# Attention and two expert layers in one kernel: the stores of weight operands leave SP's queue one slot later, behind the reads of transposed probabilities

## The chip, the cores and the metric

The kernel runs on one core of a Trainium2 chip. The metric is the time of one execution in microseconds (us), of which a lower one is better. Three runs of the kernel before gave a median of 992.63 us (991.09 to 993.33).

The engines are named as the profile names them: PE multiplies matrices (PEld is its weight load), DVE, ACT and POOL work on vectors, SP issues nearly all DMAs. SP's queue is served in order: an issue that waits holds up all issues behind it.

## The reference

The reference chains three parts. Attention in chunks of 32 queries over 8 memory keys and a window of keys (16 to the left, 8 to the right), for 4 batches, 8 heads, 768 positions, 64 numbers per head; then a layer with a cosine gate; then a layer with the maximum of three products.

```python
scores = scale * np.matmul(q_c, k_full.transpose(0, 1, 3, 2))
a = np.exp(scores - np.max(scores, axis=-1, keepdims=True))
a = a / (np.sum(a, axis=-1, keepdims=True) + 1e-09)
out[:, :, c_start:c_end] = np.matmul(a, v_full)
...
h = x @ w_in                    # 3072 x 512 by 512 x 2048
g = h * np.cos(h)
x = g @ w_out                   # back to 512
...
h = np.maximum(np.maximum(x @ w1, x @ w2), x @ w3)   # 512 to 768
return h @ w_out2
```

## The kernel before, in words

**Operands.** An fp32 product is made of three passes: each operand is split into a high part (an ACT copy to a shorter type) and the rest (a subtraction on DVE or POOL), and PE adds high by high, high by rest and rest by high (`PASSES`, `products`, line 393). So each weight needs an ACT and a DVE or POOL instruction before PE can use it, and the pair is 512 KB.

**Blocks and slots.** The 3072 tokens are 6 blocks of 512 (`j`). A block has 16 slots (`f`), one for each 128 hidden units of the first layer. In slot `s`, PE first makes `h` of that slot (`p1`, 12 matmuls). Then `chain` turns `h` into `g`: ACT (line 451), DVE (453, 454), ACT's sine (456), DVE (458), ACT (462), POOL (463); in block 0 a slightly different chain (lines 430 to 448). Then PE adds the product of `g` of slot `s - 2` with `w_out` into four banks `acc` (`p2`, 12 matmuls, in early slots of block 0 four). `g` thus has two slots of time to come about.

**Attention rides along.** While block `j` is in its slots, the attention of block `j + 1` is computed, in four units of 128 queries (numbers 0 to 3). The steps of a unit are put into slots by three tables of strings: `FIRST` for block 0, `SECOND` for block 1, `STEADY` for blocks 2 to 4. A string such as `9: "V0 T1 N2"` says what is done in slot 9:

- `S`: scores (`a_scores`, 16 + 16 matmuls, line 246, two banks of the pool `ps_a`), mask and maximum on DVE, and the load of a later unit's q and k;
- `E`: two units' exponentials on ACT (with a table load);
- `N`: row sums and reciprocals on DVE, the scaling on POOL (line 282);
- `T` (`a_t`): a DVE transpose in 32 x 32 squares (line 286, 0.97 us), and a store of the 384 KB to memory (`ptd`, line 287);
- `L` or `l` (`a_l`): three DMAs (line 292) that read them back from `ptd` in the order that PE needs, into the tile `pt`. There is one buffer for `pt`, so a load waits until the `V` before it has read it;
- `V` (`a_v`): the product with v (line 306, 16 + 16 matmuls into one bank `s`), its split into the block's `x` on ACT (308) and DVE (309), and the load of a later v (line 239).

There are two buffers in `ps_h` (tag `h`) and two in `ps_a` (tag `a`); `h` of a slot lies in `ps_h`. In `SECOND` the bank of `V` comes from `ps_h`, elsewhere from `ps_a`.

**Stores of weight operands.** `w_split` (line 203 on) splits w_in and w_out in block 0, two weights in a slot, and stores eight of the pairs (`wad`, line 211), since the buffers don't hold all 16; `wa_fetch` (line 412) brings them back in each later block. From slot 27 on, `prep_go` prepares the second layer's weights (nine groups of four operands, `q_split`, and six of `w_out2`, `o_steps`), through `store` (lines 542 to 546): ACT copy, DVE or POOL subtraction, DMA to `wd` or `wod`. `store` takes its tile from the pool `pre`, which has four buffers that also hold the group's two raw weights. Blocks of the second layer (`quad`, `b_out`) follow after slot 95 and fetch `wd` and `wod`.

**What sets the order.** A function `slot(s)` calls everything in the order of a slot: `wa_fetch`, `p1`, `chain` (with the `T` and `L` of the slot as its argument `turned`, called behind the DVE step that ends the use of `h`), and then `S`, `E`, `N`, `l` and `V` of the table with `p2`. PE and SP execute in exactly this order (`keep`, `hold`); on DVE, ACT and POOL a scheduler may move instructions that aren't kept in place. An SP issue of line 211 or 546 stands where the split is called, so it waits for the DVE or POOL instruction just ahead of it.

Of the kernel before, what the change touches and what calls it, by code (L numbers as in the profile page):

```python
# [9 lines left out]
F32 = mybir.dt.float32  # L10
# [21 lines left out]
ND = NB * S // (2 * QU)  # L32
# [3 lines left out]
DB = N // (2 * QU)  # L36
# [10 lines left out]

FIRST = {2: "S0", 3: "S1", 4: "S2", 5: "S3 E01", 6: "E23 N0", 7: "T0 N1", 8: "L0", 9: "V0 T1 N2", 10: "L1 N3", 11: "V1 T2", 12: "L2 T3", 13: "V2 l3", 14: "V3"}  # L50
SECOND = {0: "S0", 1: "S1", 2: "E01 S2", 3: "N0", 4: "S3 T0", 5: "E23 N1 L0", 6: "V0 S4 N2", 7: "T1", 8: "L1 N3", 9: "V1 S5 T2", 10: "L2 E45", 11: "V2 S6 T3", 12: "L3", 13: "V3 S7", 14: "E67"}
STEADY = {1: "N0", 2: "T0 N1", 3: "L0", 4: "S4", 5: "V0 T1 N2", 6: "L1", 7: "S5", 8: "V1 T2 N3", 9: "L2 E45", 10: "S6 T3", 11: "V2 l3", 12: "S7", 13: "V3", 14: "E67"}


# [23 lines left out]
def attn_moe_kernel(ctx, tc, qT, kT, vw, w_in, w_out, w3, w2o, out):  # L78
# [3 lines left out]
    keep = tc.keep_in_program_order  # L82
# [118 lines left out]
    def w_split(key, eng):  # L201
        c = wst.pop(key)
        w = wp.tile([128, 2, 512], F32R, tag="w", name="w")
        live[0] += 1
        assert live[0] <= NW
        keep(ACT.activation(out=w[:, 0, :], in_=c, func=AF.Copy))
        keep(eng.tensor_tensor(w[:, 1, :], c, w[:, 0, :].bitcast(F32), op=ALU.subtract))  # L207
        live[0] -= key[0] != "out" or key[1] >= PLAIN or key[1] % 2 and key[1] < PLAIN - 1
        DST[key[0]][key[1]] = (w[:, 0, :], w[:, 1, :])
        if key[0] == "out" and key[1] >= RES:  # L210
            SP.dma_start(out=wad[key[1]], in_=w.rearrange("p a c -> p (a c)").bitcast(F32))


    qk, vt, ss, sm, pt = {}, {}, {}, {}, {}
# [69 lines left out]
    def a_t(d):  # L284
        m = sm[d]
        keep(DVE.transpose(m, m))
        keep(SP.dma_start(out=ptd[d % 2], in_=m))
# [7 lines left out]
    def a_v(d):  # L295
        p, v = pt[d], vt[d]
        j, o = divmod(d, DB)
        if o == 0:
            xT[j] = xp.tile([128, 2, 4, N], F32R, tag="x", name="x")
        x = xT[j][:, :, :, 128 * o:128 * o + 128]  # L300
        late = not 2 * DB <= d < 3 * DB
        s = (ps_a if late else ps_h).tile([128, 4, 128], F32, tag="a" if late else "h", name="s")
        for t in range(2):
            for h in range(H):
                p0 = 64 * (h % 2)
                keep(PE.matmul(s[p0:p0 + 64, h // 2, QU * t:QU * t + QU], lhsT=v[:KU, t, 64 * h:64 * h + 64],  # L306
                               rhs=p[:KU, 2 * (h % 2):2 * (h % 2) + 2, 4 * t + h // 2, :], start=True, stop=True))
        ACT.activation(out=x[:, 0], in_=s, func=AF.Copy)
        DVE.tensor_tensor(x[:, 1], s, x[:, 0].bitcast(F32), op=ALU.subtract)
# [85 lines left out]
    def p1(j, f):  # L395
        if f % 2 and (done[0] or j == 0 and f == 1):
            h = ps_a.tile([128, N], F32, tag="a", name="h")
        else:
            h = ps_h.tile([128, N], F32, tag="h", name="h")
        w, x = wA_in[f], xT[j]  # L400
        for k in range(4):
            products(h, w, k, [x[:, i, k, :] for i in range(2)], k == 0, k == 3)
        live[0] -= j == NBLK - 1
        hq[j, f] = h
# [20 lines left out]
    def chain(j, f, fill, turned):  # L425
        h = hq.pop((j, f))
        ki = tr.tile([128, N], I32, tag="r", name="ki")
        c = ki.bitcast(F32)
        if j == 0:
            ACT.activation(out=ki, in_=h, func=AF.Copy, scale=INV2PI)  # L430
            DVE.scalar_tensor_tensor(c, h, INV2PI, ki, op0=ALU.mult, op1=ALU.subtract)
            fill("d0")
            fill("a0")
            ACT.activation(out=c, in_=c, func=AF.Sin, scale=math.pi)
            ACT.activation(out=c, in_=c, func=AF.Square)
            fill("a1")
            if f < PLAIN:
                g = g_t[j, f] = g_tile(F32)
                DVE.scalar_tensor_tensor(g[:, 0, :], c, 0.5, h, op0=ALU.subtract, op1=ALU.mult)
                for fn, d in turned:  # L440
                    fn(d)
            else:
                g = g_t[j, f] = g_tile()
                DVE.scalar_tensor_tensor(c, c, 0.5, h, op0=ALU.subtract, op1=ALU.mult)
                for fn, d in turned:
                    fn(d)
                ACT.activation(out=g[:, 0, :], in_=c, func=AF.Copy)
                POOL.tensor_tensor(g[:, 1, :], c, g[:, 0, :].bitcast(F32), op=ALU.subtract)
            fill("z")
            return  # L450
        row(ACT.activation(out=ki, in_=h, func=AF.Copy, scale=INV2PI, bias=0.25))  # L451
        fill("a0")
        row(DVE.scalar_tensor_tensor(c, h, INV2PI, ki, op0=ALU.mult, op1=ALU.subtract))  # L453
        row(DVE.tensor_scalar(c, c, -0.75, 0.25, op0=ALU.max, op1=ALU.min))  # L454
        fill("d0")
        row(ACT.activation(out=c, in_=c, func=AF.Sin, scale=2 * math.pi, bias=pio2))  # L456
        fill("a1")
        row(DVE.tensor_tensor(c, h, c, op=ALU.mult))  # L458
        for fn, d in turned:
            fn(d)  # L460
        g = g_tile()
        row(ACT.activation(out=g[:, 0, :], in_=c, func=AF.Copy))  # L462
        row(POOL.tensor_tensor(g[:, 1, :], c, g[:, 0, :].bitcast(F32), op=ALU.subtract))  # L463
        fill("z")
        g_t[j, f] = g
# [70 lines left out]
    def q_split(q, i, eng):  # L536
# [2 lines left out]
        n = 512 if i < 3 else 256  # L539
        store(src, n, eng, wd[q][i])  # L540

    def store(src, n, eng, dst):
        w = pre.tile([128, 2, n], F32R, tag="p", name="wq")
        keep(ACT.activation(out=w[:, 0, :], in_=src, func=AF.Copy))  # L544
        keep(eng.tensor_tensor(w[:, 1, :], src, w[:, 0, :].bitcast(F32), op=ALU.subtract))  # L545
        keep(SP.dma_start(out=dst, in_=w.rearrange("p a c -> p (a c)").bitcast(F32)))

    def q_fetch(p, q):
        for i in range(4):
# [322 lines left out]
    def slot(s):  # L872
        j, f = slots[s]
# [12 lines left out]
        def fill(where):  # L886
# [19 lines left out]
            elif where == "z":  # L906
                dec.bits()
                dec.exp(dec.nb + 2)
                dec.load()

        while wf[0] < min(s + (3 if s >= turn else 2), total):
            wa_fetch(*slots[wf[0]])
            wf[0] += 1
        p1(j, f)
        moved = [op for op in todo if op[0] in "TL" and base + int(op[1:]) < ND]
        chain(j, f, fill, [((a_t, a_l)["TL".index(op[0])], base + int(op[1:])) for op in moved])

        def do2():
            while n2[0] <= s - LOOK:
# [35 lines left out]
    for s in range(total):  # L955
        if s == turn:
            att_cm.__exit__(None, None, None)
            tmp_open("ph2", 2)
            done[0] = True
        slot(s)  # L960
        if s < PINNED:
            hold()
        else:
            hold(only=(PE.engine, SP.engine) if s < turn else (PE.engine,))
    hold(False)
    got = [AHEAD]

# [98 lines left out]
```

## Time and profile before

| | |
|---|---|
| median of 3 runs | 992.63 us (991.09 to 993.33) |
| profiled execution, its own time | 992.27 us |
| span of the profiled execution | 990.5 us |
| PE busy | 968.6 us (98%), 5426 matmuls |
| DVE busy | 555.8 us (56%) |
| ACT busy | 440.4 us (44%) |
| POOL busy | 394.4 us (40%) |
| mean granted clock of PE | 0.998 of full speed |
| moved by DMA | 186.01 MB, 188 GB/s |

The profile is of one execution; its own time is 1.77 us more than its span, and 0.36 us under the median. "Busy" is summed over instructions. A row of a timeline gives the start, the length, engine, line, operation and tiles, and in brackets how long the engine had been idle and what ended that. An idle time that is put down to a DMA is the time until its data had landed.

### The profile page before, as it was taken

The page shows a single profiled execution, that of the slowest core. Times are in us where ns is not written, and L with a number is a line of the kernel's source. Part 1 is how long each engine was busy: PE and PEld are TensorE (multiplying, and loading weights), DVE is VectorE, ACT ScalarE, POOL GpSimd, SP SyncE. Part 2 cuts the span into 40 slices and gives each one's busy share as a digit, 9 for nine tenths or more (in the row PEclk, how much of TensorE's full clock was granted, in tenths as well). Part 3 has the DMA queues.
Part 4 walks back from the last instruction along what each step waited for, and adds up shares of the span by engine and source line. Part 5 has one row for each costly group of instructions (what it writes and reads, how often), then busy time and mean ns, then how long its engine had stood idle before and what let it go on. Part 6 is the DMA issues. An engine that isn't in the chain of part 4 may idle for free.

```text
span 990.5 us, 14443 instructions
## 1 busy us (share of the span) xinstructions
PE 968.6 (98%) x5426; PEld 781.4 (79%) x5427; DVE 555.8 (56%) x840; ACT 440.4 (44%) x758; POOL 394.4 (40%) x314
## 2 busy tenths in 40 slices
PE   8998999999999999989999999999999999999998
PEld 5665778788888788878888888888888888888886
DVE  7687846564667656656655464545371455524440
ACT  6566645545445554455544454433242333323320
POOL 3565435443354445355442233333351343324320
PEclk9999999999999999999999999999999999999999
DMA  9985543456557754773577467586625655165101
GB/s 256 338 314 191 176 133 119 139 168 183 192 177 231 251 191 149 221 242 125 178 242 259 153 223 276 168 320 202 203 84 196 207 185 198 74 235 181 42 22 65
DMA packets 67413, 186.01 MB, mean 188 GB/s; under 512 B 7568, under 2 KB 15504, under 8 KB 67344
## 3 DMA queue, kind: packets, MB, share of 16 engines
q1 hardware_dynamic: 67200, 184.96, 56.1%
q8 instruction: 43, 0.70, 0.3%
q14 instruction: 26, 0.21, 0.1%
q10 hardware_dynamic: 144, 0.13, 0.0%
HBM read 140.76 MB, written 44.30 MB: 187 GB/s over the span
## 4 chain that ended last, share of the span: by engine, by line
PE 80%; DVE 6%; DMA 4%; ACT 4%; issue 3%; POOL 1%; SPq 1%; ACTq 0%; POOLq 0%; DVEq 0%
PE hb L690 26%; PE h L393 21%; PE acc L393 17%; PE hb L788 10%; DMA pt<-ptd 3%; PE s L246 2%; PE s L306 2%; PE acc L390 1%; DMA v<-in_vw_dram 1%; DVE raw L198 1%; SPq L292 1%; DVE w L207 1%; DVE ki L458 1%; DVE ki L453 1%; POOL g L463 1%
## 5 line engine op out<-in xcount | busy, mean ns | idle before, releaser
L393 PE MATMUL h<-x,w 128*128 128x512 f32 x1152 | 284.8, 397 | 1.9 <-DVE ki L458 1.9
L393 PEld LDWEIGHTS h<-x,w 128*128 128x128 f32 x1152 | 214.5, 189 | 50.9 <-DVE ki L458 2.2
L463 POOL TENSOR_TENSOR g<-ki,g 128x512 fp32r<-128x512 f32 x80 | 107.2, 1339 | 230.7 <-ACT g L462 197.0
L690 PE MATMUL hb<-x,wq 128*128 128x512 f32 x648 | 155.6, 389 | 0.0
L690 PEld LDWEIGHTS hb<-x,wq 128*128 128x128 f32 x648 | 121.6, 188 | 25.3
L393 PE MATMUL acc<-g,w 128*128 128x512 f32 x576 | 138.4, 389 | 0.0
L393 PEld LDWEIGHTS acc<-g,w 128*128 128x128 f32 x576 | 108.1, 188 | 22.5
L690 PE MATMUL hb<-xo,wq 128*128 128x512 f32 x486 | 119.1, 389 | 0.0
L393 PE MATMUL acc<-g,wa 128*128 128x512 f32 x480 | 115.9, 390 | 1.6 <-POOL g L463 1.6
L393 PEld LDWEIGHTS acc<-g,wa 128*128 128x128 f32 x480 | 89.9, 188 | 21.1 <-POOL g L463 2.5
L690 PEld LDWEIGHTS hb<-xo,wq 128*128 128x128 f32 x486 | 91.2, 188 | 18.9
L456 ACT ACTIVATE ki<-ki,pio 128x512 f32<-128x512 f32 x80 | 57.9, 723 | 106.8 <-DVE ki L454 106.7
L788 PE MATMUL hb<-wo,g 128*128 128x512 f32 x432 | 98.4, 389 | 0.0
L453 DVE SCALAR_TENSOR_TENSOR ki<-h,ki 128x512 f32<-128x512 f32 x80 | 55.0, 687 | 72.5 <-ACT ki L451 72.4
L788 PEld LDWEIGHTS hb<-wo,g 128*128 128x128 f32 x432 | 81.1, 188 | 16.8
L714 POOL TENSOR_TENSOR p<-p,p 128x512 f32<-128x512 f32 x27 | 34.8, 1290 | 130.6 <-ACT p L711 130.6
L458 DVE TENSOR_TENSOR ki<-h,ki 128x512 f32<-128x512 f32 x80 | 55.2, 690 | 56.1 <-ACT ki L456 56.1
L462 ACT ACTIVATE g<-ki 128x512 fp32r<-128x512 f32 x80 | 50.5, 631 | 58.9 <-DVE ki L458 58.9
L451 ACT ACTIVATE ki<-h 128x512 int32<-128x512 f32 x80 | 47.1, 589 | 63.2 <-PE h L393 57.8
L714 DVE TENSOR_TENSOR a<-a,hb 128x512 f32<-128x512 f32 x27 | 18.6, 688 | 93.8 <-PE hb L690 93.8
L545 DVE TENSOR_TENSOR wq<-raw,wq 128x512 fp32r<-128x512 f32 x33 | 41.2, 1266 | 24.8 <-ACT wq L544 23.5
L198 DVE SCALAR_TENSOR_TENSOR raw<-raw,top 128x512 int32<-128x512 int32 x48 | 44.2, 920 | 18.4 <-ACT top L181 13.3
(113 smaller groups left out, 1115.2 us busy)
## 6 DMA issues: line engine op xcount, KB each, us to landing
wq<-wd SPq DMA_DIRECT2D x81, 512.0 KB, 4.7
wa<-wad SPq DMA_DIRECT2D x40, 512.0 KB, 5.9
wd<-wq SPq DMA_DIRECT2D x27, 512.0 KB, 2.7
v<-in_vw_dram SPq DMA_DIRECT2D x24, 384.0 KB, 5.3
raw<-in_w_dram SPq DMA_DIRECT2D x18, 511.8 KB, 5.9
raw<-in_w_in_dram SPq DMA_DIRECT2D x16, 511.8 KB, 10.2
raw<-in_w_out_dram SPq DMA_DIRECT2D x16, 511.8 KB, 10.2
k<-in_kT_dram SPq DMA_DIRECT2D x24, 320.0 KB, 4.6
```

The source lines that it names most:

```text
L198: keep(DVE.scalar_tensor_tensor(o, z, 13, top[key], op0=ALU.logical_shift_right, op1=ALU.bitwise_or))
L393: PE.matmul(o, lhsT=w[a][:, sl], rhs=x[b], start=first and n == 0, stop=last and n == 2)
L451: row(ACT.activation(out=ki, in_=h, func=AF.Copy, scale=INV2PI, bias=0.25))
L453: row(DVE.scalar_tensor_tensor(c, h, INV2PI, ki, op0=ALU.mult, op1=ALU.subtract))
L456: row(ACT.activation(out=c, in_=c, func=AF.Sin, scale=2 * math.pi, bias=pio2))
L458: row(DVE.tensor_tensor(c, h, c, op=ALU.mult))
L462: row(ACT.activation(out=g[:, 0, :], in_=c, func=AF.Copy))
L463: row(POOL.tensor_tensor(g[:, 1, :], c, g[:, 0, :].bitcast(F32), op=ALU.subtract))
L545: keep(eng.tensor_tensor(w[:, 1, :], src, w[:, 0, :].bitcast(F32), op=ALU.subtract))
L690: keep(PE.matmul(o, lhsT=w[:, a, 256 * half + 128 * c:256 * half + 128 * c + 128], rhs=x[c][:, b, :], start=first and n == 0, stop=n == 5, ...
L714: keep(eng.tensor_tensor(o, a, b, op=op))
L788: keep(PE.matmul(o, lhsT=g[:, i, 128 * m:128 * m + 128], rhs=w[k], start=(f == 0 and n == 0), stop=(f == FB - 1 and n == 2)))
```

## The change

Four things are changed.

1. `a_l` of the table's `L` is called at the start of its slot, ahead of `wa_fetch` and `p1`, instead of within `chain`. `l` stays behind `V`.
2. The DMA of a weight store isn't issued where the operand is split, but put on a list, `later`; `flush()` issues the list in the next slot, behind that slot's `L` and `wa_fetch` and ahead of `p1` (and a last time after the last slot).
3. In `FIRST` and `SECOND` steps are moved by one to three slots, and in `FIRST` `L1` and `L2` become `l1` and `l2`. `STEADY` is as before.
4. `V` takes its bank from `ps_a` in all blocks.

```diff
-FIRST = {2: "S0", 3: "S1", 4: "S2", 5: "S3 E01", 6: "E23 N0", 7: "T0 N1", 8: "L0", 9: "V0 T1 N2", 10: "L1 N3", 11: "V1 T2", 12: "L2 T3", 13: "V2 l3", 14: "V3"}
-SECOND = {0: "S0", 1: "S1", 2: "E01 S2", 3: "N0", 4: "S3 T0", 5: "E23 N1 L0", 6: "V0 S4 N2", 7: "T1", 8: "L1 N3", 9: "V1 S5 T2", 10: "L2 E45", 11: "V2 S6 T3", 12: "L3", 13: "V3 S7", 14: "E67"}
+FIRST = {2: "S0", 3: "S1", 4: "S2", 5: "S3 E01", 6: "E23 N0", 7: "T0 N1", 8: "L0 T1 N2", 9: "V0 l1 T2", 10: "V1 l2 N3", 11: "T3", 12: "V2 l3", 14: "V3"}
+SECOND = {0: "S0", 1: "S1", 2: "E01 S2", 3: "N0 S3", 4: "T0", 5: "E23 N1 L0 S4", 6: "V0 T1", 7: "L1 N2", 8: "S5 T2 N3", 9: "V1 E45", 10: "L2 S6 T3", 11: "V2", 12: "L3 S7", 13: "V3", 14: "E67"}
 STEADY = {1: "N0", 2: "T0 N1", 3: "L0", 4: "S4", 5: "V0 T1 N2", 6: "L1", 7: "S5", 8: "V1 T2 N3", 9: "L2 E45", 10: "S6 T3", 11: "V2 l3", 12: "S7", 13: "V3", 14: "E67"}
...
         if key[0] == "out" and key[1] >= RES:
-            SP.dma_start(out=wad[key[1]], in_=w.rearrange("p a c -> p (a c)").bitcast(F32))
+            later.append((wad[key[1]], w.rearrange("p a c -> p (a c)").bitcast(F32)))
...
-        late = not 2 * DB <= d < 3 * DB
-        s = (ps_a if late else ps_h).tile([128, 4, 128], F32, tag="a" if late else "h", name="s")
+        s = ps_a.tile([128, 4, 128], F32, tag="a", name="s")
...
+    later = []
+
+    def flush():
+        while later:
+            out, in_ = later.pop(0)
+            keep(SP.dma_start(out=out, in_=in_))
...
         keep(eng.tensor_tensor(w[:, 1, :], src, w[:, 0, :].bitcast(F32), op=ALU.subtract))
-        keep(SP.dma_start(out=dst, in_=w.rearrange("p a c -> p (a c)").bitcast(F32)))
+        later.append((dst, w.rearrange("p a c -> p (a c)").bitcast(F32)))
...
+        for op in todo:
+            if op[0] == "L" and base + int(op[1:]) < ND:
+                a_l(base + int(op[1:]))
         while wf[0] < min(s + (3 if s >= turn else 2), total):
             wa_fetch(*slots[wf[0]])
             wf[0] += 1
+        flush()
         p1(j, f)
-        moved = [op for op in todo if op[0] in "TL" and base + int(op[1:]) < ND]
-        chain(j, f, fill, [((a_t, a_l)["TL".index(op[0])], base + int(op[1:])) for op in moved])
+        chain(j, f, fill, [base + int(op[1:]) for op in todo if op[0] == "T" and base + int(op[1:]) < ND])
```

What this does to the order, at three places.

SP in block 0, from the store of unit 0's transpose on (`ptd_108` and `ptd_109` are the two buffers in memory, used in turn; `raw` are loads of weights). Before:

```order
L287 DMA ptd_108<-sm 128x768
L169 DMA raw<-in_w_in_dram 128x2047
L169 DMA raw<-in_w_out_dram 128x2047
L211 DMA wad_100<-w 128x1024
L292 DMA pt<-ptd_108 32x4x256 x3
L169 DMA raw<-in_w_in_dram 128x2047
L169 DMA raw<-in_w_out_dram 128x2047
L211 DMA wad_101<-w 128x1024
L287 DMA ptd_109<-sm 128x768
L239 DMA v<-in_vw_dram 96x1024
L211 DMA wad_102<-w 128x1024
L292 DMA pt<-ptd_109 32x4x256 x3
```

and now:

```order
L287 DMA ptd_108<-sm 128x768
L169 DMA raw<-in_w_in_dram 128x2047
L169 DMA raw<-in_w_out_dram 128x2047
L292 DMA pt<-ptd_108 32x4x256 x3
L287 DMA ptd_109<-sm 128x768
L169 DMA raw<-in_w_in_dram 128x2047
L169 DMA raw<-in_w_out_dram 128x2047
L546 DMA wad_100<-w 128x1024
L287 DMA ptd_108<-sm 128x768
L239 DMA v<-in_vw_dram 96x1024
L292 DMA pt<-ptd_109 32x4x256 x3
```

The reads of `pt` of units 0 and 1 no longer stand behind a `wad` store; the store of unit 1's transpose has moved ahead of two weight loads, and that of unit 2 ahead of unit 1's read.

SP in block 2, from the store of unit 3's transpose to its read (`wd_0` to `wd_3` are one group of the second layer's operands). Before:

```order
L287 DMA ptd_109<-sm 128x768
L546 DMA wd_0_118<-wq 128x1024
L230 DMA q<-in_qT_dram 128x512
L231 DMA k<-in_kT_dram 128x640
L412 DMA wa<-wad_104 128x1024
L546 DMA wd_1_119<-wq 128x1024
L546 DMA wd_2_120<-wq 128x1024
L239 DMA v<-in_vw_dram 96x1024
L292 DMA pt<-ptd_109 32x4x256 x3
L412 DMA wa<-wad_105 128x1024
```

and now:

```order
L287 DMA ptd_109<-sm 128x768
L230 DMA q<-in_qT_dram 128x512
L231 DMA k<-in_kT_dram 128x640
L411 DMA wa<-wad_104 128x1024
L546 DMA wd_0_118<-wq 128x1024
L239 DMA v<-in_vw_dram 96x1024
L292 DMA pt<-ptd_109 32x4x256 x3
L411 DMA wa<-wad_105 128x1024
L546 DMA wd_1_119<-wq 128x1024
L546 DMA wd_2_120<-wq 128x1024
```

Two stores, `wd_1` and `wd_2`, have moved from ahead of the read to behind it, and `wd_0` stands nearer to it. `STEADY` is unchanged, so this is `flush` alone.

PE in block 1 at unit 0's `V` (line 306, 305 in the changed kernel) and the scores of the unit after the next (line 246). Before:

```order
L393 MATMUL h<-x,w 128x512 x12
L393 MATMUL acc_1623<-g,w 128x512 x3
L393 MATMUL acc_1624<-g,w 128x512 x3
L393 MATMUL acc_1625<-g,w 128x512 x3
L393 MATMUL acc_1626<-g,w 128x512 x3
L306 MATMUL s<-pt,v 64x64 x16
L246 MATMUL s<-k,q 64x96 x16
L393 MATMUL h<-x,w 128x512 x12
```

and now:

```order
L246 MATMUL s<-k,q 64x96 x16
L392 MATMUL h<-x,w 128x512 x12
L392 MATMUL acc_1623<-g,w 128x512 x3
L392 MATMUL acc_1624<-g,w 128x512 x3
L392 MATMUL acc_1625<-g,w 128x512 x3
L392 MATMUL acc_1626<-g,w 128x512 x3
L305 MATMUL s<-pt,v 64x64 x16
L392 MATMUL h<-x,w 128x512 x12
```

The scores stand a slot ahead of `V` instead of right behind it. PE's instructions are the same in number and size throughout; only such steps change places.

## Rows read from the trace of the kernel before

**Rows 1.** The page's head and its first row on PE (section 1).

```profile
span 990.5 us, 14443 instructions
PE 968.6 (98%) x5426; PEld 781.4 (79%) x5427; DVE 555.8 (56%) x840; ACT 440.4 (44%) x758; POOL 394.4 (40%) x314
```

**Rows 2.** Waits of PE over the span: us in total, times, longest us.

```profile
PE s L306 <- DMA pt<-ptd: 8.7, 7, 2.8
PE h L393 <- DVE ki L458: 1.9, 2, 1.3
PE acc L393 <- POOL g L463: 1.6, 2, 1.3
```

**Rows 3.** Timeline of PE in block 0: V0 to V3, and h after V0.

```profile
93.55 1.15 PE L306 MATMUL s<-pt,v 96*64 96x64 f32 x32 [2.82 <-DMA pt<-ptd]
94.63 4.62 PE L393 MATMUL h<-x,w 128*128 128x512 f32 x12
...
108.34 1.15 PE L306 MATMUL s<-pt,v 96*64 96x64 f32 x32 [0.91 <-DMA pt<-ptd]
...
121.19 1.15 PE L306 MATMUL s<-pt,v 96*64 96x64 f32 x32 [0.59 <-DMA pt<-ptd]
...
129.15 1.15 PE L306 MATMUL s<-pt,v 96*64 96x64 f32 x32 [1.13 <-DMA pt<-ptd]
```

**Rows 4.** Busy time by stretch, granted clock (PEclk), DMA share, GB/s: block 0.

```profile
90.00:100.00 10.00, 7.18 (x50) 5.30 (x49) 4.63 (x6) 3.68 (x7) 3.97 (x4) 0.83 0.83 282
91.00:130.00 39.00, 33.83 (x245) 27.44 (x247) 29.05 (x33) 23.51 (x41) 17.49 (x15) 0.96 0.68 224
```

**Rows 5.** Timeline of PE in blocks 1 to 3: stalls, and h after the longest.

```profile
184.83 3.02 PE L393 MATMUL h<-x,w 128*128 128x512 f32 x12 [1.26 <-DVE ki L458]
...
229.97 1.15 PE L306 MATMUL s<-pt,v 96*64 96x64 f32 x32 [0.55 <-DMA pt<-ptd]
...
331.55 1.15 PE L306 MATMUL s<-pt,v 96*64 96x64 f32 x32 [0.84 <-DMA pt<-ptd]
...
434.30 1.15 PE L306 MATMUL s<-pt,v 96*64 96x64 f32 x32 [1.88 <-DMA pt<-ptd]
435.38 3.02 PE L393 MATMUL h<-x,w 128*128 128x512 f32 x12
```

**Rows 6.** Timeline of SP in block 0.

```profile
81.50 0.33 SPq L287 DMA_DIRECT2D ptd<-sm  x1
...
88.02 0.33 SPq L211 DMA_DIRECT2D wad<-w  x1
88.45 1.74 SPq L292 DMA_DIRECT2D pt<-ptd  x3
...
122.84 0.37 SPq L239 DMA_DIRECT2D v<-in_vw_dram  x1
123.39 1.63 SPq L292 DMA_DIRECT2D pt<-ptd  x3
```

**Rows 7.** DMA issues: KB each, median us from issue to landing.

```profile
ptd<-sm SPq DMA_DIRECT2D x20, 384.0 KB, 2.6
wd<-wq SPq DMA_DIRECT2D x27, 512.0 KB, 2.7
```

**Rows 8.** Timeline of DVE in block 0: transpose of unit 1.

```profile
90.62 0.97 DVE L286 STREAM_TRANSPOSE sm<-sm 128x768 f32<-128x768 f32 x1
```

**Rows 9.** Timeline of SP in block 2, ahead of unit 3's read.

```profile
323.02 1.34 SPq L546 DMA_DIRECT2D wd<-wq  x2
...
324.90 2.01 SPq L292 DMA_DIRECT2D pt<-ptd  x3
```

**Rows 10.** ACT's copy of an operand to be stored: count, busy, mean ns, idle before.

```profile
L544 ACT ACTIVATE wq<-raw 128x512 fp32r<-128x512 f32 x33 | 20.9, 655 | 2.9 <-DVE raw L198 1.6 <-POOL raw L522 1.0 <-issue 0.4
```

**Rows 11.** Timeline of POOL in block 3: a g.

```profile
399.47 1.29 POOL L463 TENSOR_TENSOR g<-ki,g 128x512 fp32r<-128x512 f32 x1 [2.51 <-ACT g L462]
```

**Rows 12.** Timeline of PE in block 3: the product that uses this g.

```profile
406.85 2.88 PE L393 MATMUL acc<-g,wa 128*128 128x512 f32 x12
```

More of the change, by code (lines that the diff above doesn't have):

```diff
@@ L439, in chain @@
                 DVE.scalar_tensor_tensor(g[:, 0, :], c, 0.5, h, op0=ALU.subtract, op1=ALU.mult)
-                for fn, d in turned:
-                    fn(d)
+                for d in turned:
+                    a_t(d)
             else:
@@ L444, in chain @@
                 DVE.scalar_tensor_tensor(c, c, 0.5, h, op0=ALU.subtract, op1=ALU.mult)
-                for fn, d in turned:
-                    fn(d)
+                for d in turned:
+                    a_t(d)
                 ACT.activation(out=g[:, 0, :], in_=c, func=AF.Copy)
@@ L458, in chain @@
         row(DVE.tensor_tensor(c, h, c, op=ALU.mult))
-        for fn, d in turned:
-            fn(d)
+        for d in turned:
+            a_t(d)
         g = g_tile()
@@ L964, in attn_moe_kernel @@
             hold(only=(PE.engine, SP.engine) if s < turn else (PE.engine,))
+    flush()
     hold(False)
```

## The prediction
> **What bounds the kernel now.** I read the page first: PE is busy for 968.6 of 990.5 us [rows 1], and the change leaves the number and sizes of its matmuls alone. So only PE's idle time can be won, 21.9 us in all, together with stretches in which its clock is low. I then asked for PE's waits [rows 2]: 8.7 us for `pt` ahead of `V`, 1.9 us for DVE ahead of `h`, 1.6 us for POOL's g; the rest of the idle time lies in the start-up and at the end, where nothing is changed. Then I looked up each stall in PE's timeline: four ahead of `V0` to `V3` in block 0, of 2.82, 0.91, 0.59 and 1.13 us [rows 3], and one each in blocks 1, 2 and 3, of 0.55, 0.84 and 1.88 us [rows 5]. The longest has a sequel: the 12 matmuls of `h` behind it took 4.62 us [rows 3] against 3.02 us elsewhere [rows 5], which is 1.60 us more, and the mean granted clock of those ten microseconds was 0.83 [rows 4], so part of them ran at 1.2 instead of 2.4 GHz. No other stall has such a sequel; the `h` behind the stall of 1.88 us took 3.02 us [rows 5]. Last, SP's timeline says why the reads are late. In block 0 the transpose was on its way at 81.50, but the read left at 88.45, right behind the `wad` store at 88.02, which had waited for its DVE split [rows 6].
>
> **The change, part by part.** The profiled execution took 992.27 us, 0.36 us less than the median of the runs, so I work out a difference and take it from the median.
>
> *V0 in block 0.* The read now stands ahead of the `wad` store. The transpose's store left at 81.50 and a store of this kind lands after 2.6 us [rows 6, 7], so the read can leave at 84.1 instead of 88.45. From the first issue to the start of `V0` it was 93.55 - 88.45 = 5.1 us [rows 3, 6], so the data is there at 89.2. PE was free at 93.55 - 2.82 = 90.73. The stall goes, with 1.5 us to spare, and the slow clock that followed it: 2.82 + 1.60 = 4.42 us.
>
> *V1 in block 0* moves from slot 11 to slot 10, one slot behind `V0`. Its read can only leave once `V0` has emptied the single `pt` buffer, and the load of v stands ahead of it. That is what `V3` had before: the `V` ahead of it ended at 121.19 + 1.15 = 122.34, v left at 122.84, the read at 123.39, and `V3` began at 129.15, after a stall of 1.13 us [rows 3, 6]. So the old stall of 0.91 us goes and one of some 1.13 us comes. Its lower bound is 0; its upper one is `V0`'s old loss, 4.42 us. I take 1.13, since the pattern is the same. Unit 2's transpose and its store also stand ahead of this read; unit 1's transpose, 0.97 us of DVE [rows 8], now lies ahead of it on DVE too, which speaks for a little more, while the 512 KB `wad` store that stood ahead of `V3`'s read is gone, which speaks for less. The Trainium skill (DMA: Bandwidth & Descriptors, Specifications) gives a core about 358 GB/s of HBM; by my estimate from that figure v and the read, 768 KB, need 2.2 us, the read is in time, and the forecast below would be 980.4 us. `V3`'s 5.8 us from the read's issue to the start of `V` [rows 3, 6] contradicts this, and I keep to the rows.
>
> *V2 and V3 in block 0* now have two slots between them and the `V` ahead. A slot without attention takes about 5.5 us (h of 3.02 and acc of 2.88 us, which overlap a little [rows 5, 12]), so the read has some 11 us where 6.8 us were needed (122.34 to 129.15). Both stalls go: 0.59 + 1.13 = 1.72 us.
>
> *Block 1.* With `V` in `ps_a`, `h` no longer has to share its two banks. The two stalls of `h` on DVE, 1.9 us together [rows 2], of which 1.26 us stand at 184.83 [rows 5], lie right behind a `V` with scores in `SECOND`; both go. `V` and the scores now share `ps_a`, but stand a slot apart, so the readers of a bank (ACT 308 and DVE 309, or DVE 263) have about 5.5 us; I cost that at nothing, with the 1.9 us of the same kind of wait as its upper bound. `V3`'s 0.55 us goes too: the transpose of unit 3 is a slot earlier, and its read ahead of `wa_fetch`. Together 2.45 us.
>
> *Blocks 2 to 4.* In block 2 the read of unit 3 left at 324.90, behind two `wd` stores that had left only at 323.02, when their DVE halves were done; `V3` began 6.65 us after the read's issue, 0.84 us late [rows 5, 9]. The two stores now stand behind the read, and what is left ahead of it, `wd_0`, is a slot old. The read then waits only for `V2`, which is over some 5 us earlier. The same pattern stood in block 3, with 1.88 us [rows 5]. Together 2.72 us.
>
> *What is added or moved at no cost.* The later stores keep a buffer of `pre` for up to a slot longer; ACT's copies into that pool have waited for no DMA so far (2.9 us of idle time, all for DVE, POOL or issue) [rows 10]. Cover: a g that POOL finished at 400.76 was used at 406.85 [rows 11, 12], so ACT may lose some 6 us in one place before PE notices. Without that cover each group would cost what is in the third rival. On SP the `L` reads now hold up `wa_fetch` and the stores until the transpose has landed; `wa` is used two slots later. On DVE and POOL the moved transposes, row sums and scalings are the same work a slot earlier or later; its cover is the same lag. The waits of PE for POOL, 1.6 us [rows 2], I leave as they are; they may go, which is the lower end.
>
> **The sum**: 4.42 + 0.91 - 1.13 + 1.72 + 2.45 + 2.72 = 11.1 us. 992.63 - 11.1 = **981.5 us**.
>
> **The rivals.**
>
> *The stall moves to V1 with its slow clock.* If the read of unit 1 is as late as `V0`'s was, PE loses 4.42 us there instead of 1.13, and the time is 984.8 us. For it: v, 384 KB, and a store of 384 KB lie ahead of the read in a stretch in which the DMA engines are 83% busy [rows 4]. Against it: `V3` managed with 1.13 us. The Trainium skill (TensorE: Matmul & The Clock Gate, Part 1: The HAM clock gate) says that the clock is throttled by default, that activity releases it, and that the monitor runs free of the kernel, so that the same stall may cost the clock in one place and not in another; by that rule a stall of 1.13 us could bring the 1.60 us alone, and 983.1 us. The trace shows the one fall, and none behind the stall of 1.88 us [rows 5].
>
> *DVE becomes the bound in block 0.* From 91 to 130 us DVE is busy for 29.05 of 39.0 us, PE for 33.83 [rows 4]. Without its stalls PE needs the stretch in about 34 us, and DVE would be 85% busy, with ACT and POOL between its steps. If three slots there each come late by a transpose and a split of x that moved forward (0.97 + 0.69 us), 5.0 us come back: 986.5 us. Against it: the new table spreads the transposes and `V`s more evenly, and only 1.9 us of PE's waits are for DVE, none of them in block 0 [rows 2].
>
> *Slower: the stores starve `pre`.* If a store that left at once now leaves a slot later (5.5 us) and lands after 2.7 us [rows 7], ACT's next copy into the pool can wait 8.2 us; g has 6.1 us [rows 11, 12]. Each such wait then costs PE 2.1 us. It decides from the point where a `wd` store leaves more than 3.4 us later than before. With two a group and nine groups that is 38 us, and even after the gain of 11.1 us the time would be near 1019 us; with one a group it is 19 us and 1000.4 us, which I take for this rival. Against it: a store had to wait for its DVE or POOL half anyway, so most of the slot is no delay.
>
> *The change doesn't do what it says.* The reads stand earlier in the queue, but wait there for the transpose to land or for the one `pt` buffer, and come as late as before. Then only the 1.9 us of `h` is won: 990.7 us. Against it: in block 0 the `wad` store left 0.43 us ahead of the read [rows 6], so it was the store that held it.
>
> **How the numbers follow.** The forecast gets 0.61, the stall at `V1` 0.15, DVE in block 0 0.12, no effect 0.07, slower 0.05. The lower end is the forecast without `V1`'s stall and without the waits for POOL: 981.5 - 1.13 - 1.6 = 978.8, rounded to 979. The upper end takes in the first two rivals and stops at 987, which leaves out the last two and a little of each tail, less than 2 in 10. A measurement of this kernel can tell about 0.2%, or 2.0 us, from no change. Faster by more than that are the forecast and the first two rivals, 0.88; within it is "no effect", 0.07; slower 0.05.
>
> **What would show it.** Right: no wait for `pt` at `V0`, `V2` and `V3` in block 0 nor in blocks 1 to 3; one of about 1 us at `V1`; `h` behind `V0` at 3.0 us and the granted clock at 1.00 from 90 to 100 us; no wait of `h` for DVE in block 1; PE's busy time lower by about 1.6 us, its idle time by about 9.5 us. Wrong: a stall of over 2 us at `V1`, with a slow `h` behind it; new waits of PE for DVE between 90 and 130 us; copies into `pre` that wait for a DMA, with waits for POOL's g behind them in blocks 1 to 3.

## The result, and the profile after

The changed kernel takes **983.39 us** (median of 6 runs, 980.98 to 987.27), the kernel before 992.01 us (6 runs, 991.09 to 993.33). The ratio is 0.9915, with a 95% interval of 0.9894 to 0.9936: faster by 8.6 us, where 11.1 us were forecast. The profiled execution took 984.24 us, with a span of 982.4 us, 8.1 us less than that of before.

The head of the page after, as in [rows 1]:

```profile
span 982.4 us, 14452 instructions
PE 970.9 (99%) x5427; PEld 782.8 (80%) x5427; DVE 554.4 (56%) x840; ACT 440.7 (45%) x758; POOL 393.4 (40%) x314
```

PE's idle time fell from 21.9 to 11.5 us, by 10.4 us, but its busy time rose by 2.3 us, with the same matmuls. So idle time was won, and clock was lost. The longest wait of PE after:

```profile
PE s L305 <- DMA pt<-ptd: 3.3, 1, 3.3
```

Of the 12.2 us of [rows 2] this one wait is left, of 3.33 us; all others belong to the start-up. Where it stands, in PE's timeline of block 0, beside [rows 3]:

```profile
89.72 1.15 PE L305 MATMUL s<-pt,v 96*64 96x64 f32 x32
90.81 3.02 PE L392 MATMUL h<-x,w 128*128 128x512 f32 x12
...
99.88 1.97 PE L305 MATMUL s<-pt,v 96*64 96x64 f32 x32 [3.33 <-DMA pt<-ptd]
101.78 5.17 PE L392 MATMUL h<-x,w 128*128 128x512 f32 x12
...
115.08 1.15 PE L305 MATMUL s<-pt,v 96*64 96x64 f32 x32
...
127.27 1.15 PE L305 MATMUL s<-pt,v 96*64 96x64 f32 x32
```

These are `V0` to `V3`. `V0`, `V2` and `V3` no longer wait, and `h` behind `V0` takes its 3.02 us. `V1` waits, and now `V1` itself and the `h` behind it are slow: 0.82 and 2.15 us longer than elsewhere. Busy time by stretch, before and then after (columns as in [rows 4]):

```profile
90.00:130.00 40.00, 34.56 (x247) 27.44 (x247) 30.04 (x34) 23.77 (x41) 17.78 (x16) 0.96 0.69 225
130.00:430.00 300.00, 295.47 (x1994) 241.04 (x1990) 183.37 (x288) 149.77 (x227) 135.97 (x108) 1.00 0.56 178
```

```profile
90.00:130.00 40.00, 36.67 (x254) 29.87 (x250) 27.91 (x35) 25.10 (x43) 18.22 (x15) 0.91 0.61 186
130.00:430.00 300.00, 300.00 (x2030) 244.03 (x2029) 186.56 (x294) 152.95 (x232) 140.56 (x112) 1.00 0.59 188
```

From 130 to 430 us, blocks 1 to 3 without the last stall of before at 434.30, PE had 4.5 us of idle time and now has none. In block 0 the mean granted clock has fallen from 0.96 to 0.91, so PE spent more of that stretch at 1.2 instead of 2.4 GHz: this is the one place seen where the change costs something. SP's timeline there, as in [rows 6]:

```profile
80.56 0.33 SPq L287 DMA_DIRECT2D ptd<-sm  x1
...
83.61 1.29 SPq L292 DMA_DIRECT2D pt<-ptd  x3
85.67 0.34 SPq L287 DMA_DIRECT2D ptd<-sm  x1
...
87.14 0.40 SPq L546 DMA_DIRECT2D wad<-w  x1
92.32 0.33 SPq L287 DMA_DIRECT2D ptd<-sm  x1
92.70 0.42 SPq L239 DMA_DIRECT2D v<-in_vw_dram  x1
93.17 1.50 SPq L292 DMA_DIRECT2D pt<-ptd  x3
94.77 0.38 SPq L546 DMA_DIRECT2D wad<-w  x1
```

Unit 0's read leaves at 83.61, 3.05 us behind its store, and no longer 6.95 us behind it. Unit 1's transpose is stored at 85.67, but its read leaves only at 93.17: `V0` was over at 89.72 + 1.15 = 90.87, then SP stood at the store of unit 2's transpose until 92.32, and v went ahead too. (A `wad` store still stands ahead of unit 1's read as well, but it left at 87.14, 6 us before.) DVE's timeline says what that store waited for:

```profile
91.28 0.97 DVE L286 STREAM_TRANSPOSE sm<-sm 128x768 f32<-128x768 f32 x1
```

The transpose of unit 2 ended at 92.25, 1.38 us behind `V0`.

### The profile page after: what moved, and what is told of

It reads as the page before. It is cut to its first block, busy times and chain, and to the rows that moved or that the text cites. A ratio compares the mean times of both kernels' runs of the same rounds, so it can differ in the third digit from the quotient of the medians.

```text
span 982.4 us, 14452 instructions
## 1 busy us (share of the span) xinstructions
PE 970.9 (99%) x5427; PEld 782.8 (80%) x5427; DVE 554.4 (56%) x840; ACT 440.7 (45%) x758; POOL 393.4 (40%) x314
## 4 chain that ended last, share of the span: by engine, by line
PE 91%; DVE 3%; DMA 2%; ACT 2%; issue 1%; SPq 0%; POOL 0%; ACTq 0%; DVEq 0%; POOLq 0%
PE hb L696 26%; PE h L392 25%; PE acc L392 22%; PE hb L794 10%; PE s L246 3%; PE s L305 2%; PE acc L389 1%; DMA raw<-in_w2o_dram 1%; DMA pt<-ptd 1%; PE warm L375 1%; DMA raw<-in_w_out_dram 1%; DVE raw L198 1%; PE s L356 0%; ACT top L181 0%; DVE sm L286 0%
```

## The experiments

Two theories stood against each other for what is lost at `V1`. One: the single `pt` buffer lets the read start only behind `V0`, and what stands between (unit 2's store, which waits for DVE, and v) adds the rest. The other: the DMA engines are full in this stretch, and the read is late wherever it stands. A second question was which of the four parts of the change makes the gain. Kernels are grouped by question; each is compared with runs of before on its own chip, whose medians were 989.89 us (e1 to e4), 991.80 us (e0, e5, the first run of e7, e8) and 989.82 us (the second run of e7, e9 to e11). Each profile shows one of a kernel's executions.

### The stall at V1

**e1: a buffer of its own for unit 1.** Unit 1's `pt` lies in the pool `pre`, and its read can leave at the start of slot 9, ahead of `V0`.

```diff
-... 9: "V0 l1 T2", ...
+... 9: "V0 L1 T2", ...
-        pt[d] = t2.tile([128, 4, H, 32], F32, tag="pt", name="pt", bufs=1)
+        if d == DB + 1:
+            pt[d] = pre.tile([128, 4, H, 32], F32, tag="p", name="pt")
+        else:
+            pt[d] = t2.tile([128, 4, H, 32], F32, tag="pt", name="pt", bufs=1)
```

> The changed kernel, but unit 1 of block 0 has a pt buffer of its own (a free tile of pre), and its read stands at the start of slot 9 instead of behind V0. Theory (V1's stall of 3.33 us, with 3.0 us of slow clock behind it, comes from the single pt buffer, which lets the read leave only after V0): no wait for pt at V1, granted clock 1.00 from 90 to 110 us, 6.3 us less than the changed kernel's profiled span of 982.4, so a span near 976 and a time near 978 us. Rival A (the DMA traffic of block 0 makes the read late wherever it stands): V1 still waits 1 us or more, a time of 981 to 984 us. Rival B (DVE is next in line in block 0): no wait for pt, but new waits of PE for DVE or POOL between 95 and 125 us that take back over 2 us.

It took 976.90 us (976.60 to 978.24), ratio 0.9871 [0.9847, 0.9894]. SP's timeline, the read of unit 1, and PE's, `V1`:

```profile
88.43 1.27 SPq L295 DMA_DIRECT2D pt<-ptd  x3
```

```profile
95.49 1.15 PE L308 MATMUL s<-pt,v 96*64 96x64 f32 x32
96.57 2.99 PE L395 MATMUL h<-x,w 128*128 128x512 f32 x12
```

The read leaves 0.31 us ahead of the start of `V0` (88.74), where in the changed kernel it left 3.45 us behind it; there is no stall and no low clock, and the mean granted clock is 1.00. The DMA engines are as full as in the changed kernel, with a share of 1.02 from 88.43 to 95.49, and the three parts of the read land 3.6 to 3.8 us after their issue. So the read isn't late wherever it stands.

**e2: the read ahead of v.** `l` is called in front of `V`'s load of v; unit 2's store still stands ahead.

```diff
-                a_l(d)
+                pass
...
+                for l in todo:
+                    if l[0] == "l" and base + int(l[1:]) < ND:
+                        a_l(base + int(l[1:]))
```

> The changed kernel, but where V is followed by l, the read of pt is issued ahead of the load of a later v instead of behind it. Theory (what stands ahead of the read counts): the read leaves 0.4 us earlier and without 384 KB ahead of it, lands some 1.5 us earlier, V1's stall falls from 3.33 to under 2.2 us, and the slow clock behind it may go too: 979 to 982 us. Rival A (the traffic that was issued before, two loads of weights and two stores, sets the landing): the stall stays within 0.5 us of 3.33, no change in time.

It took 982.07 us (978.95 to 984.82), ratio 0.9919 [0.9888, 0.9951]. Its profiled execution was the shortest of the four, 978.95 us:

```profile
98.16 1.15 PE L305 MATMUL s<-pt,v 96*64 96x64 f32 x32 [1.72 <-DMA pt<-ptd]
99.24 3.02 PE L392 MATMUL h<-x,w 128*128 128x512 f32 x12
```

Half of the stall is left, and here no low clock follows it. In the three other executions the mean granted clock was 0.998, 0.998 and 0.995, and they took 3.0 to 5.9 us longer; where their clock was low isn't known. So the median alone, close to the changed kernel's, would have said that v is of no account.

**e3: unit 2's transpose a slot later.** Its store then stands behind unit 1's read.

```diff
-... 9: "V0 l1 T2", 10: "V1 l2 N3", ...
+... 9: "V0 l1", 10: "V1 T2 l2 N3", ...
```

> The changed kernel with T2 in slot 10 instead of slot 9, so that the store of unit 2's transpose no longer stands ahead of unit 1's read. Theory: v and the read leave once V0 is over, at about 91.0 instead of 92.7 and 93.2 us, so the read lands 1.4 us or more earlier, and V1's stall falls to 2 us or less: 979 to 982 us. V2 in slot 12 must stay without a wait. Rival A (traffic): the read leaves earlier but lands at about the same time; stall over 2.8 us.

It took 978.17 us (977.35 to 979.18), ratio 0.9878 [0.9851, 0.9905], a little less than expected.

```profile
98.38 1.15 PE L305 MATMUL s<-pt,v 96*64 96x64 f32 x32 [0.63 <-DMA pt<-ptd]
99.47 3.02 PE L392 MATMUL h<-x,w 128*128 128x512 f32 x12
```

Where the reads left is in SP's timeline; that of e3, then of e2:

```profile
92.12 0.34 SPq L239 DMA_DIRECT2D v<-in_vw_dram  x1
92.64 1.27 SPq L292 DMA_DIRECT2D pt<-ptd  x3
```

```profile
92.63 1.47 SPq L292 DMA_DIRECT2D pt<-ptd  x3
```

The three kernels can be set side by side with `V3` of before, which the prediction took as its pattern, and with `V3` of e9 (below), which has the old table but later stores. In before a `wad` store of 512 KB stood ahead of that read too, just before v:

```profile
122.40 0.34 SPq L211 DMA_DIRECT2D wad<-w  x1
```

All have some 5.7 us of PE's work between the two `V`s, so the stall is the sum of two pieces less 5.7 us.

| | end of the `V` ahead to the read's first issue | that to the next `V` | issued between the `V` ahead and the read | stall |
|---|---|---|---|---|
| before, `V3` | 1.05 | 5.76 | `wad` store, v | 1.13 |
| e9, `V3` | 0.56 | 5.38 | v | 0.28 |
| changed, `V1` | 2.30 | 6.71 | unit 2's store, v | 3.33 |
| e2, `V1` | 1.86 | 5.53 | unit 2's store | 1.72 |
| e3, `V1` | 0.56 | 5.74 | v | 0.63 |

The changed kernel loses 1.25 us more than `V3` did before its read starts, and 0.95 us more until the data is used, together the 2.20 us between 1.13 and 3.33. The first piece is unit 2's store, which stands until its transpose is done: without that store it is 0.56 us (e3). The second piece isn't explained by the bytes just ahead alone. Among the three kernels with `V1` in slot 10 it is 5.5 and 5.7 us behind one 384 KB transfer, v or the store, and 6.7 us behind both. But `V3` of before had 896 KB just ahead of its read and needed 5.76 us. It also had less traffic in the 6 us ahead of the read, a DMA share of 0.62 against 0.99 (before, then after):

```profile
117.39:123.39 6.00, 5.41 (x52) 4.31 (x51) 6.00 (x7) 4.43 (x9) 3.72 (x3) 1.00 0.62 201
87.17:93.17 6.00, 6.00 (x49) 3.83 (x48) 5.36 (x6) 3.03 (x6) 2.83 (x3) 1.00 0.99 330
```

So the theory that the read is late wherever it stands falls with e1, but what earlier traffic and the transfers just ahead each add to the second piece is not separated by these runs.

### Which part makes the gain

**e7: the changed kernel with the old `FIRST`.**

```diff
-FIRST = {... 7: "T0 N1", 8: "L0 T1 N2", 9: "V0 l1 T2", 10: "V1 l2 N3", 11: "T3", 12: "V2 l3", 14: "V3"}
+FIRST = {... 7: "T0 N1", 8: "L0", 9: "V0 T1 N2", 10: "L1 N3", 11: "V1 T2", 12: "L2 T3", 13: "V2 l3", 14: "V3"}
```

> The changed kernel with the old FIRST. The run with the old tables and banks had no stall over 0.3 us at V0 to V3 in block 0 and lost 2.5 us at h in block 1 and 1.6 us ahead of one unit's scores. Theory (the moves in FIRST cost V1's stall and win nothing that the later stores don't win): no stall over 0.5 us in block 0 and none in block 1, 1 to 4 us less than with both old tables, 4 to 6 us less than the changed kernel on the same chip: about 976 to 979 us. Rival (V3 behind V2 with l3 between them stalls again as soon as block 1 changes): 980 us or more.

> The changed kernel with the old FIRST once more, beside the three others on one chip. Theory: no wait of PE over 0.6 us between 30 and 640 us, granted clock 1.00, 13 to 15 us less than the kernel before, and a spread of under 2 us between executions, since there is no stall that the clock could fall behind. Rival (the chip of the first run was a good one): less than 11 us.

It took 977.14 us (976.77 to 978.37) and, on another chip, 977.18 us (976.22 to 977.81); ratios 0.9844 [0.9829, 0.9859] and 0.9878 [0.9855, 0.99]. The page of the second:

```profile
span 975.7 us, 14453 instructions
PE 967.3 (99%) x5426; PEld 779.9 (80%) x5427; DVE 556.6 (57%) x840; ACT 440.4 (45%) x758; POOL 393.5 (40%) x314
```

This run gained 12.6 us, a little less than the 13 to 15 expected, because before was faster on this chip; the first gained 14.7. Of the second's waits behind the start-up one of 0.2 us is left. In block 0, busy time by stretch:

```profile
90.00:124.00 34.00, 33.96 (x241) 27.65 (x238) 29.17 (x34) 23.52 (x41) 18.63 (x15) 1.00 0.70 225
```

PE is idle for 0.04 us there, with DVE 86% busy. **This kernel beats both before and the changed kernel**, and e1 does as well: the new `FIRST` isn't only of no use, it is what costs the stall.

**e0: the changed kernel once more**, beside e7 on its chip.

> The changed kernel once more, on the chip of the three others, so that they are compared under the same conditions. Theory (V1's stall of over 3 us is the kernel's and not one execution's): PE waits 2.5 us or more for pt at V1, followed by a granted clock below 1.00 in some of the executions, and a spread of several us between executions. Rival (a chance of that execution): no wait over 1.5 us.

It took 982.50 us (980.43 to 983.54), ratio 0.9889 [0.987, 0.9908], so e7 is faster by 5.4 us on the same chip. Its `V1` waited 3.40 us, and `h` behind it took 4.60 us, while `V1` itself ran in its 1.15 us. So the stall is the kernel's; the loss of clock behind it differs between executions.

**e9: the later stores alone.** Tables, banks and the place of the reads are those of before; `later` and `flush` are those of the change.

```diff
-            SP.dma_start(out=wad[key[1]], in_=w.rearrange("p a c -> p (a c)").bitcast(F32))
+            later.append((wad[key[1]], w.rearrange("p a c -> p (a c)").bitcast(F32)))
...
-        keep(SP.dma_start(out=dst, in_=w.rearrange("p a c -> p (a c)").bitcast(F32)))
+        later.append((dst, w.rearrange("p a c -> p (a c)").bitcast(F32)))
...
+        flush()
         p1(j, f)
```

> The later stores alone: old tables and banks, and the reads of L within chain as before. Theory (the later stores are the part that carries the gain; moving the read to the start of its slot adds little): no wait for pt over 0.5 us at V0 nor at units 3 of blocks 2 and 3, at V1 at most 1 us, since a store of slot 9 stands ahead of its read, and 8 to 11 us less than before on the same chip. Rival (both halves are needed in block 0): V0 or V1 waits over 2 us, less than 6 us gained.

It took 979.10 us (978.72 to 979.64), ratio 0.9896 [0.9871, 0.9922]. The waits of PE that are not the start-up's:

```profile
PE h L393 <- DVE ki L458: 1.9, 2, 1.3
...
PE s L306 <- DMA pt<-ptd: 0.3, 1, 0.3
PE s L306 <- PE acc L393: 0.2, 1, 0.2
```

Of [rows 2] the 8.7 us for `pt` are down to 0.3, POOL's 1.6 are gone, and the two waits of `h` in block 1 stand as they were. The later stores alone bring 10.7 us; e7 brings 1.9 us more on this chip, the size of the two waits. `V3` of block 0, one slot behind `V2` as in before, waits 0.28 us where it waited 1.13.

**e4: later stores and early reads**, with the old tables and banks (e9, and `L` at the start of the slot).

> The later stores and the reads at the start of their slot alone: FIRST, SECOND and the banks are those of the kernel before. By the prediction's terms V0's stall and slow clock go (4.42 us), the stalls of units 3 in blocks 2 and 3 go (2.72 us), V1 to V3 of block 0 keep at least V3's 1.13 us (one slot behind V2), and the two stalls of h in block 1 (1.9 us) stay: about 983 to 985 us. Rival (the new tables carry the gain, and a read at the start of its slot waits there for what it waited for before): V0 still waits over 2 us, time 989 us or more.

It took 980.87 us (978.32 to 982.38), ratio 0.9905 [0.9878, 0.9933], with no wait for `pt` at all. So my expectation, 983 to 985 us with 1.13 us left at `V3`, was too high. The early reads add nothing that can be seen to e9's gain; its waits of `h` were 2.5 us, and a wait of scores for DVE, 1.6 us, is new.

**e8: early reads alone**, stores at once, old tables and banks.

```diff
+        for op in todo:
+            if op[0] == "L" and base + int(op[1:]) < ND:
+                a_l(base + int(op[1:]))
         while wf[0] < min(s + (3 if s >= turn else 2), total):
...
-        moved = [op for op in todo if op[0] in "TL" and base + int(op[1:]) < ND]
+        moved = [op for op in todo if op[0] in "T" and base + int(op[1:]) < ND]
```

> The kernel before with the reads of L at the start of their slot and nothing else: stores at once, old tables and banks. Theory (in block 0 it is the read's place that counts, since the store ahead of V0's read was issued in the same slot; in blocks 2 and 3, where the read is an l, only the later stores help): V0's stall and slow clock gone, the stalls of units 3 in blocks 2 and 3 still there, 4 to 6 us less than before on the same chip. Rival (the later stores are needed everywhere): V0 still waits over 2 us, and the time is that of before.

It took 987.87 us (984.00 to 988.74), ratio 0.9937 [0.9917, 0.9957]. That is 3.9 us less than before, just short of the 4 to 6 expected. `V0` has no wait; the waits for `pt` that are left are those of `V3` in block 0, 2.06 us, and in block 3, 1.63 us. In PE's timeline of block 0:

```profile
123.12 1.15 PE L306 MATMUL s<-pt,v 96*64 96x64 f32 x32 [2.06 <-DMA pt<-ptd]
124.21 4.60 PE L393 MATMUL h<-x,w 128*128 128x512 f32 x12
```

This part heals the units whose read is an `L` (0 to 2 in block 0, 3 in block 1). The reads of units 3 in blocks 0 and 3 are an `l` and stand behind `wad` and `wd` stores as before; they keep their stalls, and the slow `h` turns up at `V3` of block 0. In block 2, where the stall was expected to stay, 0.32 us are left, which the profile puts down to no DMA.

**e5: tables and banks alone**, stores at once and reads in `chain`.

> The new tables FIRST and SECOND and the banks from ps_a alone; stores are issued at once and the reads of L stand within chain, as in the kernel before. Theory (the stores ahead of the reads made V0's stall and those in blocks 2 and 3; the tables only take the two stalls of h in block 1 and V2's and V3's in block 0, and bring V1's): V0 waits 2 us or more, V1 3 us or more, the stalls of units 3 in blocks 2 and 3 stay, no wait of h for DVE in block 1; within 3 us of the kernel before on the same chip. Rival (the tables carry the gain): 5 us or more faster than before.

It took 991.37 us (10 runs, 986.03 to 993.85), ratio 0.9991 [0.9972, 1.001]: no gain. Its waits of PE and the place of the longest:

```profile
PE s L306 <- DMA pt<-ptd: 9.0, 4, 4.3
```

```profile
91.04 1.15 PE L306 MATMUL s<-pt,v 96*64 96x64 f32 x32 [2.12 <-DMA pt<-ptd]
92.12 3.02 PE L393 MATMUL h<-x,w 128*128 128x512 f32 x12
...
102.14 1.98 PE L306 MATMUL s<-pt,v 96*64 96x64 f32 x32 [4.28 <-DMA pt<-ptd]
104.05 4.72 PE L393 MATMUL h<-x,w 128*128 128x512 f32 x12
...
431.88 1.90 PE L306 MATMUL s<-pt,v 96*64 96x64 f32 x32 [2.27 <-DMA pt<-ptd]
```

The tables take away the waits of `h` in block 1 and those of `V2` and `V3` in block 0, and give it all back at `V1`. Block 3's stall stays, 2.27 us, and is gone with the later stores alone (e9): that one is the stores'. Block 2's, which was expected to stay, is down to 0.29 us.

### The bank of V in block 1

**e10: e7 with `V` of block 1 in `ps_h`, as before.**

```diff
-        s = ps_a.tile([128, 4, 128], F32, tag="a", name="s")
+        late = not 2 * DB <= d < 3 * DB
+        s = (ps_a if late else ps_h).tile([128, 4, 128], F32, tag="a" if late else "h", name="s")
```

> The changed kernel with the old FIRST, and with the bank of V in block 1 from ps_h as before; SECOND is the new one. Theory (sharing ps_h with V is what made h wait in block 1): two to four waits of h for DVE in block 1, 1 to 3 us in all, and as much more time than the same kernel with ps_a. Rival (the scores behind V in the same slot kept DVE from freeing the bank, so that the new table alone cures it): no wait of h over 0.3 us and the same time.

It took 978.55 us (977.66 to 979.01), ratio 0.9891 [0.9869, 0.9913], and PE's waits hold none of `h` for DVE. My theory, that only the bank takes these waits away, falls: the scores no longer stand right behind `V` in `SECOND`, and that alone does it. The median is 1.4 us above e7's on this chip; the profiles show no cause for it in block 1, but a start 0.53 us later and a wait for POOL's g at 583.09 us of 0.85 us, where e7 has 0.18.

**e11: e7 with the old `SECOND` too, `V` staying in `ps_a`.**

> Old FIRST and old SECOND with the later stores, and the bank of V in block 1 from ps_a. Theory (V and scores of one slot can't share the two banks of ps_a without a wait, so the bank and the table had to change together): no wait of h for DVE, but scores in block 1 that wait for ACT's and DVE's readers of V's bank, three or four times about 1.3 us, so 2 to 5 us more than with the new SECOND. Rival (the bank alone cures block 1): no wait of the scores over 0.5 us and the time of the kernel with the new SECOND.

It took 980.79 us (980.07 to 982.33), ratio 0.9917 [0.9893, 0.994]. The waits of PE in block 1:

```profile
PE s L246 <- DVE x L309: 1.4, 2, 0.8
PE s L246 <- DVE sm L263: 1.3, 2, 0.7
```

There are four waits, as expected, of 0.66 to 0.75 us, half the expected size. The kernel takes 3.6 us more than e7, within the 2 to 5 expected. With the old table the bank in `ps_a` only moves the wait from `h` to the scores, and makes it 2.7 us instead of 1.9. So the new table does the work with either bank, and the bank does nothing without the table.

## Why the prediction was right, and where it was off

The direction and the range were right, and so was the mechanism: reads freed of the stores ahead of them. The time came out 1.9 us above the forecast. That it came so near is in part luck: `V1` cost 5.2 us more than its term, and 2.5 us that the sum had at nothing came back elsewhere, 0.93 of them by chance (the start-up, below). The prediction's own first sign of being wrong, a stall of over 2 us at `V1` with a slow `h` behind it, came true. By its own terms, on the profiled spans (us, minus is faster):

| term | forecast | measured |
|---|---|---|
| `V0` in block 0, stall and slow `h` | -4.42 | -4.42 |
| `V1`, old stall | -0.91 | -0.91 |
| `V1`, new stall and clock | +1.13 | +6.34 |
| `V2` and `V3` in block 0 | -1.72 | -1.72 |
| block 1 | -2.45 | -2.45 |
| blocks 2 and 3 | -2.72 | -2.72 |
| waits for POOL | 0 | -1.6 |
| start-up | 0 | -0.93 |
| sum | -11.1 | -8.4 (spans: -8.1) |

*`V1`* is the step that failed: "I take 1.13, since the pattern is the same". The 6.34 us are 3.33 of stall, 0.82 of a slow `V`, 2.15 of a slow `h` and 0.04 of the product behind it. It lies even above the upper bound of 4.42, and so does e0's 3.40 + 1.58 = 4.98. The prediction saw that unit 2's store stands ahead of the read and counted it as "a little more", against the `wad` store that is gone. The difference is when the two were ready: the `wad` store left 0.06 us behind the end of `V2` (122.40, 122.34), while unit 2's store waited for a DVE transpose that ended 1.38 us behind `V0`. Without it `V1` waits 0.63 us (e3), less than the pattern. The pattern itself held a store of the kind that the change moves: with later stores alone, `V3` waits 0.28 us (e9).

The Trainium skill (DMA: Bandwidth & Descriptors, Specifications) gives a limit of about 358 GB/s for a core's HBM traffic. The prediction's estimate from it, 2.2 us for 768 KB, isn't borne out: 6.71 us passed from the issue to the start of `V`. The DMA moved 249 GB/s in them, which is twice the 768 KB, so other transfers shared the time.

*`V0`, `V2` and `V3`* came out in size, but not all for the reasons given. For `V0` either half is enough, the read's place (e8) or the later store (e9). For `V2` and `V3` the two slots of the new table aren't needed: with the old table and later stores `V2` has no wait for `pt`, and `V3` one of 0.28 us.

*The rivals.* The first rival saw what came, the stall and its slow clock moved to `V1`, and priced it at 4.42 us where it is 6.34; with the two gains that no term had, its 984.8 us is near the result. DVE didn't become the bound: no wait for DVE in block 0 after, nor in e7, where it is 86% busy. `pre` didn't starve: ACT's copies into it after, in the view of the groups, wait for DVE alone:

```profile
L550 ACT ACTIVATE wq<-raw 128x512 fp32r<-128x512 f32 x33 | 21.0, 653 | 2.8 <-DVE raw L198 2.7
```

In e9 1.1 us of such a wait for a `wd` store do appear, and PE has no wait for POOL, so the cover held. That the change does nothing fell with `V0`.

*Block 1* came out in size, but the reason given, the bank, isn't what does it. The new table alone takes the waits of `h` away (e10); the bank alone does too, but makes the scores wait instead (e11).

*POOL's waits* were left as they are. The larger one, in block 3, is there in before, e5 and e8 (1.29, 0.71 and 0.60 us), all with stores at once, and in no profile with later stores. The smaller, later than 580 us (0.34 us in before), is gone in after, but kernels with later stores have one there too, of 0.18 to 0.85 us (e1, e7, e10), so that one can't be put down to the change. In block 3 SP's timeline suggests how it comes about. Before:

```profile
394.58 1.79 SPq L546 DMA_DIRECT2D wd<-wq  x2
396.49 0.38 SPq L230 DMA_DIRECT2D q<-in_qT_dram  x1
...
399.64 0.33 SPq L287 DMA_DIRECT2D ptd<-sm  x1
400.02 1.10 SPq L169 DMA_DIRECT2D raw<-in_w_dram  x2
```

and after:

```profile
387.49 0.33 SPq L230 DMA_DIRECT2D q<-in_qT_dram  x1
...
394.88 0.32 SPq L287 DMA_DIRECT2D ptd<-sm  x1
395.25 0.96 SPq L169 DMA_DIRECT2D raw<-in_w_dram  x2
```

Held by the `wd` stores, the loads of q, k and `wa` left 3.2 us ahead of the transpose's store; freed of them they left 7.4 us ahead of it, and no longer compete with the loads of raw weights. ACT took up the second of these 8.46 us after the issue before (at 408.48), 7.13 us after it now (at 402.38): 1.3 us sooner, the size of the wait for g that followed (1.29 us at 422.45). That this is the chain is an argument from these rows; no run tried it alone.

*The start-up* is not the change's. The first `h` came at 28.84 us before and at 27.91 after with the same order of work, at 29.12 in e0, which is the changed kernel again, and between 26.89 and 29.12 over all profiles. So the 0.93 us are a chance of the two executions. 0.3 us of the spans' difference stay open.

*PE's busy time* was to fall by 1.6 us and rose by 2.3: 2.97 us of low clock at `V1` in place of 1.60 at `V0` make 1.4 of it; the rest was not traced.

## What to carry to other kernels

In a queue that is served in order, look at each issue ahead of the one that matters and ask when *its* source is ready: stores that stood where their operand was made cost 10.7 us here, and putting them off by a slot was the cure; the new `SECOND`, the bank and the early reads together brought 1.9 us more (e7 against e9). The same look should go over a new order, since a table that pulls one store forward can put it ahead of a read that has a single buffer and one slot of time. A price taken from a similar place holds only if what stands ahead in the queue is ready as early there; fewer bytes ahead were no help here, since one of the two transfers wasn't ready.

## What the runs showed of the hardware

**The clock after a stall isn't settled by the stall's length.** `h` was slow behind stalls of 2.06 us (e8), 2.27 and 4.28 (e5), 2.82 (before), 3.33 (after) and 3.40 (e0), and `V` itself too in after and both places of e5. Behind 2.12 us in e5's block 0 both ran at full speed. In e2 the same kernel took 978.95 us with a mean granted clock of 1.00, and 984.82 us with 0.995. The Trainium skill (TensorE: Matmul & The Clock Gate, Part 1: The HAM clock gate) says that the window of the monitor behind the clock runs free and doesn't start anew with a kernel. The prediction took from this that the same stall may cost the clock in one place and not in another; these rows agree with that, but don't show the reason. For the sum it means that a stall can carry a second price, here 1.5 us (e5, block 3) to 3.0 us (after) in the six places named, and that the kernels with such a stall scattered more: 980.98 to 987.27 us for the changed kernel, 976.22 to 978.37 for e7.

**A read back from memory** took 5.4 to 6.7 us from the first of its three issues to the start of a `V` that waited for it, in the five rows of the table above. One 384 KB transfer more just ahead went with about 1 us more where the traffic before was alike (e2, e3 and after); it isn't a rule, as `V3` of before shows with 896 KB and 5.76 us.
